# A new order of all steps, with the small matrix products in longer rows of one tile shape

## The chip, the cores and the metric

The kernel runs on one core of a Trainium2 chip. The metric is the device time in microseconds (us) of one execution, as the median of several runs. The profile is one execution taken by the hardware profiler.

## The reference

Two parts follow each other. The first is a recurrence over 768 time steps for 4 x 8 heads with states of 40 x 40; the second is a feed-forward block (FFN) with an exact gelu on 3072 tokens of width 320 and an inner width of 2048. All is float32.

```python
for t in range(S):                                   # S = 768, B = 4, H = 8, D = 40
    y[:, :, t] = einsum('bhd,bhde->bhe', rt, state)
    Sa = einsum('bhde,bhe->bhd', state, at)
    state = state * wt[:, :, None, :] - einsum('bhd,bhe->bhde', Sa, bt)
    state = state + einsum('bhd,bhe->bhde', vt, kt)
x = y.transpose(0, 2, 1, 3).reshape(B * S, H * D)    # 3072 x 320
h = x @ w_in                                         # 320 x 2048
out = (0.5 * h * (1 + erf(h / sqrt(2)))) @ w_out     # 2048 x 320
```

## The kernel before

The recurrence is cut into 12 chunks of 64 steps. Within a chunk it becomes matrix products over the 32 heads (four 64-row or 64-column quarters of the TensorE array each work on another head), with the inverse of a triangular 64 x 64 matrix for each head. After each chunk its 256 tokens go through the FFN.

The kernel is a set of step functions, one for each kind of work, and each takes the chunk's number. A step is a generator: it issues a few instructions, yields, and goes on when it is called again. One long string, ORDER, names the steps by hand, token for token (`A7:2` is the next piece of step A of chunk 7, with PSUM buffer 2), and a loop calls them in that order. So ORDER sets the order of the instructions on every engine (TensorE, VectorE, ScalarE, GpSimd and the DMA queue of SyncE, called SP), and which of four PSUM buffers (duo0 to duo3, two banks each) a product uses. No scheduler changes it. Semaphores make each instruction wait for the data and the buffers that it needs; within an engine all stays in order.

```python
for token in ORDER.split():
    name, *at = token.split(":")
    places[:] = [int(x) for x in at]
    if name not in going:
        kind = name.rstrip("0123456789")
        going[name] = steps[kind](int(name[len(kind):]))
    next(going[name], None)
```

The steps of a chunk c, with the lines that stand for them in the profile:

- Loads by SP: w, a, b, k, v, r (L213, L224, L227, L239, L266, L277). Later chunks are loaded in pairs of rows, so that VectorE can turn them: L561 is its transpose, in ta, tb, tk, tv, tr and wt.
- logs, sums and wt: the decays. ScalarE takes Ln and Exp (L499, L522, L542, L547, L549), VectorE the running sum (L544, a scan).
- ta, tb, tk: operands scaled by the decays (L588 makes aT, L614 nT, L631 kT). sc and sk scale rows of b and k (L597, and L605 on GpSimd).
- N, A, RV: small products of these operands, 32 each of 64 x 64 (TensorE, L149, the helper of all small products), each masked by VectorE out of PSUM (L676).
- The inverse of N: the mask's result goes to DRAM (L715), comes back as blocks of 32 x 32 (nb, L784), GpSimd inverts them (inv, L799 and L801, 31 rounds), the result goes to DRAM (L808), and ft loads it into the tile Tt (L822, L826). Then corner (VectorE transpose L908, small products, ScalarE copy L916) and joined (small products of tile shape 32 x 32, then a copy by ScalarE and one by VectorE, both L931) fill in the missing quarter of Tt.
- av, X: small products, added up in avs (L760, L943). sa and saT multiply avs by Tt; saT's result goes to the tile late (L980, L981), sa's to SM (L968). tn transposes the state (L557, then L997), M is a masked product of late with rT.
- yy, QY, qk: 32 small products each, added up in two PSUM buffers; y multiplies them into xt (L1045) and SP moves some rows of xt (L1071, L1076); state brings the state up to date (L1091, L1092).
- ph: the first FFN product, 160 products in four pieces with the tile shape 64 x 128 (L1119), gelu by ScalarE (L1122).
- po: the second FFN product with the full shape 128 x 128. Chunks 0 and 1 take it plainly (L1141); the others by seven products of half the size (L1157) with sums by VectorE before and after (L1164, L1172, L1184, L1185, L1161) and copies by ScalarE (L1174, L1175, L1187). The result is stored by SP (L1131).

Before chunk 2 the weights, which come as 64-bit floats, are made into float32 by VectorE and ScalarE (ci and co, L457 to L473). The first chunk's inverse is made on TensorE instead (sq, cornerd, joinedd).

The tile shape of a small product is 64 x 64 rows and columns of the array, but 32 x 32 in corner and joined. A float32 product appears in the profile as two matmul records, a transpose as one.

Of the kernel before, what the change touches and what calls it, by code (L numbers as in the profile page):

```python
# [29 lines left out]
ORDER = """  # L30
w0 begin6 pads1 consts0 w1 tails1 b1 inv1 zeros1 begin6:0 logs0 zeros2 wi0 gaps0 b0 consts0 logs1 tails0 pads0 a0
consts0 sums0:1 gaps1 sums0:2 zeros0 v0 sums0 zeros4 warm6:3 pads3 pads2 sums1:0 zeros3 shifts0 sums0 sc0 a1 sums1:3
sums1 tb0:2 sums1 sc1 wi0 ta0:1 r0 tb0 ta0 tb1:3 N0:0 N0 tb1 wi0 ta1:2 k0 ta1 N0 tv0:1 sq1 v1 tv0 sq0 N1:3 sq0 sq0:0
sq1 sq0 sq1:2 k1 sq0 sq1 warm1:1 N1 sq1 sk0 ci0:0 wi0 sq1:0 N1 ci0 sq1 tr0:1 sq1 ci0 tk0:2 wi0 tk0 sk1 wi0 sq0:3 sq1
sq0 tr0 A0:2 ci1:1 sq1:0 sq0 ci1 sq1 sq0 nb1 sq1 A0 sq1 wi0 sq0:1 wi0 sq0 RV0:3 sq0 RV0 sq0 wl1 sq1:0 wl1 sq1 inv1 r2
sq0:2 sq1 sq1 sq0 tk1:1 sq0 sq0 sq1:3 tk1 w2 sq1 sq0:0 sq0 cornerd0 placed2 av0:2 ci2:2 placed3 cornerd0:3 ci1 ci2
inv1 nb1 placed1 warm0:1 cornerd0 wl0 ci3:0 wl0 av0 av0:0 r1 ci2 joinedd0:1 av0 joinedd0 tr2:3 placed0 joinedd0 tr2
warm2:2 wi1 a2 ci3 sa0:0 sa0 sa0:1 inv1 sa0 b2 warm5:2 ci4:1 ci9:2 ci4 QY0:3:0 logs2 ci4 k2 qk0 warm7:2 ci9 y0 warm3:1
wi1 state0 wi1 A1:2 wi1 A1 wi1 sums2:1 wi1 inv1 ci9 wo2 sums2:0 sums2 ci3 tv1:3 tv1 tr1:2 sc2 sums2 tn1:0 ci5:1 tn1
ta2:3 ta2 ci5 av1:1 tr1 ci5 sk2 inv1 y0:0 tb2:3 wi1 inv2 ci7:2 tb2 wo6 zeros6 y0:2 ci7 zeros7 y0 y0 tk2:3 av1 ci6:0  # L40
N2:2 ci6 N2 ft1 tk2 co3:1 ph0:0 ft1 ci6 wi1 ph0 corner1:0 N2 ci7 X1:1 corner1:2 corner1 ft1 ph0 X1 ph0:3 wo0 ci8:0
co2:2 ci8 RV1:2 RV1 nb2 warm4:1 ci8 joined1:0 wo9 joined1 wq3 ph0 co0:0 joined1 co0 inv2 ph0 co0 v2 ph0:1 co2 co3
co1:0 sa1:2 co1 sa1 w3 co1 saT1:0 saT1 co3 ph0 co2 wo4 ph0 inv2 ph0:3 co6:0 wt3:1 co6 co7:2 ph0 vp3 co7 ph0 co7
yy1:2:0 logs3 M1:1 M1 tv2:3 wt3 co6 wo8 sums3:1 nb2 sums3 wt3 QY1 zeros5 a3 inv3 tv2 qk1 co4:2 y1 wo15 po0:1 inv2
co5:0 y1 state1 co5 co4 po0 co5 RV2:3 wo10 A2:0 co4 y1 tn2:2 A2 tn2 co9:0 po0 ta3 co9 wt3 inv2 co15:2 bp3 po0 co9 co15
av2:0 co11:1 kp3 co8:0 co11 av2 co11 ph1:2 co8 co8 wo14 inv2 ph1 co10:1 tb3 co10 ph1 wo13 ph1:0 co10 a4 ph1 RV2 ph1
inv4 ft2 co14:0 ph1:2 ta3 co14 wo12 ft2 co14 ft2 N3:3 co15 X2:0 k4 X2 ph1 corner2:1 co13:0 corner2:0 N3 corner2 co13
co12:2 N3 po0 co13 co12 joined2:0 tables0 joined2 k3 joined2 po0 ta4 ph1 co12 sa2:3 nb3 tables0 saT2:0 tk3:1 b3 sa2
sk3 saT2 po0 r3 inv3 yy2:2:3 po0 po0 M2:0 po0 nb3 M2 po0 tv3 ph1:1 inv3 po0 tr3 wq4 ph1 sc3 QY2 w4 qk2 y2 po1:0 state2
bp4 inv3 po1 logs4 b4 A3:2 y2 A3 X3:3 wt4:0 po1 wt4 v3 ph1 wt4 po1 y2 inv3 wt4 po1 po1 ta4 kp4 po1 inv3 vp4 av3:2 tb4  # L50
av3 sums4:1 po1 X3 po1 RV3:2 v4 ws0 sums4 N4:3 N4 inv5 sk4 RV3 ph2:1 N4 sc4 tk4:2 ph2 ft3 ph2 ft3 ph2:3 ws3 nb4 ws1
nb4 ph2 corner3:1 ph2 ft3 ph2:2 inv4 a5 corner3:1 corner3 w5 ph2 ph2 joined3:3 joined3 r4 tn3:1 joined3 tn3 inv4
saT3:3 saT3 sa3:2 sa3 logs5 po1 ph2:1 ta5 bp5 yy3:3:2 M3:0 M3 inv4 tv4 ph2 ph2 tr4 wq5 QY3 qk3 po2:0 po1 sums5:0 sums5
y3 po1 po2:1 state3 y3 po2 inv4 wt5:2 RV4:0 po2:1 po2 wt5 k5 A4:2 po2 A4 tn4:3 y3 tn4 wt5 po2:1 tables1 wt5 po2 po2
inv4 kp5 av4:2 tb5 av4 X4:3 po2 ph3:2 sk5 X4 a6 po2 ta5 ph3 v5 RV4 N5:3 N5 ws2 po2:1 N5 po2 ft4 po2 ph3 ft4 ph3:0 ft4
corner4:0 nb5 tk5:2 ph3 vp5 ph3 corner4:3 ta6 corner4 inv5 nb5 po2 po2:1 po2 joined4:2 joined4 joined4 ph3:0 b5 saT4:3
saT4 sa4:1 r5 inv5 sa4 ph3 ph3 sc5 ph3:2 w6 yy4:3:1 M4:0 M4 tv5 ph3 inv5 ph3 tr5 wq6 QY4 logs6 po3:1 qk4 bp6 state4
po3:0 kp6 y4 po3 po3:2 wt6:0 A5:2 po2 sums6:1 A5 wt6 inv6 k6 inv5 sums6 wt6 y4 po3 wt6 po3 po3:3 po3 po3 tn5:2 y4 tn5
av5:1 tb6 RV5:0 po3 av5 po3 po3:2 ta6 b6 po3 inv5 po3 a7 N6:1 X5:3 N6 X5 N6 sk6 ph4:2 RV5 tk6:1 ph4 ph4 ft5 ta7 ph4:1
ft5 sc6 ft5 A6:3 corner5:0 nb6 r6 inv6 po3 po3:0 po3 corner5:2 A6 corner5 ph4 joined5:0 joined5 ph4 joined5 ph4:2 vp6  # L60
sa5:3 sa5 saT5:0 saT5 inv6 ph4 nb6 ph4 yy5:1:3 w7 M5:0 tr6 tv6 ph4:2 M5 wq7 ph4 inv6 ph4 QY5 v6 logs7 po4:2 qk5 po3 y5
bp7 po4:0 wt7:1 state5 wt7 po4 kp7 po4:0 av6:2 inv7 av6 y5 inv6 wt7 po4 po4 po4:1 wt7 po4 po4 v7 sums7:3 X6:2 y5 po4
ta7 sums7 tb7 po4 po4:0 po4 a8 X6 N7:3 inv6 N7 RV6:1 tk7:2 N7 ph5:2 po4 k7 ph5 ph5 ph5:3 ft6 nb7 ph5 ft6 ph5 nb7
# [22 lines left out]
y11 po10:0 y11 po10 po10 y11 po10 y11 po10 po10:2 y11 y11 y11 po10 y11 po10 po10 po10:1 po10 po10 ph11:3 ph11 ph11
ph11:0 ph11 ph11 ph11:2 ph11 ph11 ph11:1 ph11 ph11 po11:0 po11:3 po11 po11:2 po11 po11 po11:0 po11 po11 po11 po11
po11:2 po11 po11 po11 po11:1 po11 po11
# [1179 lines left out]
```

## Time and profile before

| | |
|---|---|
| runs | 662.33, 666.8 and 668.32 us; median 666.8 us |
| span of the profiled execution | 661.8 us (its own time is not listed apart from the three runs) |
| TensorE | busy 646.7 us, weight loads 567.3 us, 13768 matmuls |
| VectorE | busy 416.0 us, 536 instructions |
| ScalarE | busy 239.3 us, 305 instructions |
| GpSimd | busy 367.7 us, 799 instructions |
| DMA | 79.41 MB, queue q1 with 58.3% of 16 engines' time |

The span goes from the first to the last instruction. A busy TensorE isn't TensorE at its peak: the ends of matmuls are modelled. The granted TensorE clock was 0.999 over the span. In the rows, `<-` in a tile pair stands between what is written and what is read, and behind `<-` in an idle time stands what ended it; "duo" is any of the four PSUM buffers.

### The profile page before, as it was taken

What the parts mean: (1) busy time and instruction counts of PE and PEld (TensorE: products, weight loads), DVE (VectorE), ACT (ScalarE), POOL (GpSimd) and SP (SyncE); (2) the same over time, 40 slices, a digit from 0 to 9 for tenths busy, and PEclk for the clock granted to TensorE, in tenths of its full rate; (3) what the DMA queues carried; (4) which work ended last, traced back from release to release, by engine and by line L of the source; (5) the groups of instructions that cost most, each with busy time, mean ns of one, the idle gap of its engine ahead of it and who ended that gap; (6) DMA issues with size and microseconds to landing.
All of it is one profiled execution on the core that took longest, in us unless ns stands there. A gap on an engine that the chain in (4) does not pass through costs nothing.

```text
span 661.8 us, 30753 instructions
## 1 busy us (share of the span) xinstructions
PE 646.7 (98%) x13768; PEld 567.3 (86%) x13768; DVE 416.0 (63%) x536; ACT 239.3 (36%) x305; POOL 367.7 (56%) x799
## 2 busy tenths in 40 slices
...
GB/s 136 164 192 176 158 167 132 153 159 146 116 132 134 105 137 134 140 116 112 145 141 107 94 153 124 119 147 110 115 146 111 103 121 102 86 101 3 42 1 21
DMA packets 300708, 79.41 MB, mean 120 GB/s; under 512 B 288584, under 2 KB 293328, under 8 KB 300576
## 3 DMA queue, kind: packets, MB, share of 16 engines
q1 hardware_dynamic: 299512, 74.92, 58.3%
q0 software_dynamic: 864, 2.36, 1.8%
...
q14 instruction: 24, 0.20, 0.1%
q10 hardware_dynamic: 200, 0.16, 0.1%
...
## 4 chain that ended last, share of the span: by engine, by line
PE 82%; DVE 8%; SPq 5%; issue 2%; DMA 1%; ACT 0%; DVEq 0%; ACTq 0%
PE duo L1119 29%; PE duo L149 25%; PE duo L1157 22%; PE duo L1141 4%; PE duo L557 2%; SPq L213 2%; SPq L227 1%; DVE conv L466 1%; SPq L1076 1%; DVE conv L472 1%; DMA spare<-in_a_dram 1%; DVE conv L458 1%; DVE conv L457 1%; DVE aT L588 1%; DMA rows<-in_b_dram 0%
## 5 line engine op out<-in xcount | busy, mean ns | idle before, releaser
L1119 PE MATMUL duo<-xt,w_in_sb 64*128 64x256 f32 x1920 | 218.8, 381 | 1.4 <-issue 1.4
L1119 PEld LDWEIGHTS duo<-xt,w_in_sb 64*128 64x128 f32 x1920 | 182.5, 187 | 23.9 <-issue 2.3
L799 POOL TENSOR_TENSOR tmp<-W,Nb 128x56 f32<-128x56 f32 (+22 forms) x155 | 71.8, 464 | 79.9 <-DMA Nb<-N 51.4
L1122 ACT ACTIVATE gt<-duo 128x1024 f32<-128x1024 f32 x48 | 49.2, 1025 | 143.0 <-PE duo L1119 132.1
L799 POOL TENSOR_TENSOR tmp<-rT,Nb 128x56 f32<-128x56 f32 (+22 forms) x155 | 70.2, 453 | 52.8 <-DMA Nb<-N 41.0
L1157 PE MATMUL duo<-w_out_sb,gt 128*128 128x160 f32 x640 | 93.3, 303 | 0.0
L1157 PEld LDWEIGHTS duo<-w_out_sb,gt 128*128 128x128 f32 x640 | 87.6, 190 | 2.4 <-issue 0.8
L801 POOL TENSOR_TENSOR W<-W,tmp 128x56 f32<-128x56 f32 (+22 forms) x155 | 71.8, 463 | 12.1
L801 POOL TENSOR_TENSOR rT<-rT,tmp 128x56 f32<-128x56 f32 (+22 forms) x155 | 68.4, 441 | 12.1
L1157 PE MATMUL duo<-extra,conv 128*128 128x160 f32 x320 | 46.0, 301 | 0.0
L1157 PEld LDWEIGHTS duo<-extra,conv 128*128 128x128 f32 x320 | 43.8, 190 | 1.4 <-issue 0.5
L1141 PE MATMUL duo<-w_out_sb,gt 128*128 128x320 f32 x128 | 36.9, 440 | 0.1
L1161 DVE TENSOR_TENSOR os<-os,duo 128x160 f32<-128x160 f32 x40 | 12.7, 318 | 31.9 <-PE duo L1157 28.0
L1141 PEld LDWEIGHTS duo<-w_out_sb,gt 128*128 128x128 f32 x128 | 23.6, 190 | 10.1 <-issue 0.5
L1164 DVE TENSOR_TENSOR conv<-gt 128x1024 f32<-128x1024 f32 x10 | 12.7, 1266 | 27.5 <-ACT gt L1122 27.5
L605 POOL TENSOR_TENSOR rows<-rows,w_tile 128x640 f32<-128x640 f32 x9 | 15.8, 1761 | 25.0 <-DMA Nb<-N 16.0
L676 DVE TENSOR_TENSOR SM<-duo,left_upper 128x1024 f32<-128x1024 f32 x11 | 13.4, 1221 | 24.4 <-PE duo L149 24.4
L931 DVE COPY Tt<-duo 32x512 f32<-32x512 f32 x11 | 7.6, 689 | 30.4 <-ACT Tt L931 30.3
L149 PE MATMUL duo<-rT,late 40*64 40x64 f32 x1472 | 26.1, 219 | 0.0
L149 PEld LDWEIGHTS duo<-rT,late 40*64 40x64 f32 x1472 | 23.7, 135 | 2.1 <-issue 2.1
L1122 ACT ACT_TABLE_LOAD x14 | 18.0, 1283 | 19.1 <-DVE os L1161 14.7
L1157 PE MATMUL duo<-extra,gt 128*128 128x160 f32 x160 | 23.9, 302 | 0.0
...
## 6 DMA issues: line engine op xcount, KB each, us to landing
...
```

The costliest lines, as they stand in the source:

```text
L149: nc.tensor.matmul(o, lhsT, rhs, start=first, stop=True, skip_group_check=True)
L213: nc.sync.dma_start(out=t[half(e)].rearrange("p g h d -> p (g h) d")[:, :, :D], in_=rows_of(src, c, e))
L557: nc.tensor.transpose(pt[:, g, n], src(g, n), ident)
L605: (nc.gpsimd if c in SCALED_BY_POOL or c >= NB else nc.vector).tensor_tensor(to, raws.pop((c, "k")), t["rw"], ALU.mult)
L676: nc.vector.tensor_tensor(to, pt, upper.unsqueeze(1).to_broadcast([P, NBL, C]), ALU.mult)
L799: eng.tensor_tensor(t, W[:, :nr, j:j + 1].to_broadcast([P, nr, rest]), Nb[:, j:j + 1, j + 1:].to_broadcast([P, nr, rest]), ALU.mult)
L801: eng.tensor_tensor(W[:, :nr, j + 1:], W[:, :nr, j + 1:], t, ALU.add)
L1119: nc.tensor.matmul(pt[:, x, s], w_in_sb[half(x), kt, p * P:(p + 1) * P], xt[half(x), kt], start=kt == 0, stop=kt == NK - 1)
L1122: nc.scalar.activation(gt[:, 4 * q:4 * q + 4].rearrange("p (x s) t -> p x s t", x=2), pt, ACT.Gelu)
L1141: nc.tensor.matmul(pt[:, g], gt[:, f, g * P:(g + 1) * P], w_out_sb[:, f], start=f == 0, stop=f == NF - 1)
L1157: nc.tensor.matmul(pt[:, n, :DM // 2], l_[:, f], r_[:, f], start=f == 0, stop=f == NF // 2 - 1)
L1161: nc.vector.tensor_tensor(to, one_, other, ALU.add)
```

## The change

ORDER alone is replaced by another string of the same steps; no function changes. All steps of all chunks, and with them the instructions and DMAs of all engines, stand in another order, and many tokens have another PSUM buffer. Each step is called as often as before. Small products of one tile shape are gathered: before, single small products alternate with pieces of ph and po; after, several pieces of one step and several small products follow each other. Here is the stretch around chunk 7 in both strings; the rest is changed in the same way.

```diff
-corner6:0 ph5:0 RV6 ft6 inv7 corner6:2 po4 corner6 tn6:3 r7 tn6 po4:1 po4 joined6:2 ta8 joined6 joined6 ph5 inv7 vp7
-ph5 sa6:3 sa6 saT6:1 saT6 ph5:2 po4 yy6:0:3 bp8 M6:1 M6 inv7 tr7 ph5 ph5 tv7 QY6 po5:1 wq8 qk6 y6 po5:1 state6 y6 po5
-po5:2 inv7 po5 wt8:0 A7:2 y6 RV7:0 A7 wt8 tn7:3 RV7 tn7 wt8 vp8 inv7 po5 po5:1 po5 wt8 po5 X7:2 av7:0 inv8 av7 tb8 sk7
-kp8 po5 ta8 b7 inv9 po5 po5:3 po5 a9 po5 N8:0 N8 ft7 ph6:1 N8 ph6 ph6 ft7 ta9 ph6:3 ft7 corner7:1 X7 ph6 tk8:2 nb8 ph6
...
+X6:2 po4 N7:0 inv7 ph5:1 ph5 ph5 X6 ph5:2 inv8 sc6 N7 ph5 N7 ph5 ph5:1 ft6 ft6 corner6:1 ph5 nb7 ft6 ph5 corner6:2 vp7
+tn6:0 corner6 joined6:1 joined6 RV6:2 sk6 w7 tn6 tk7:0 inv7 ta8 inv7 r7 joined6 saT6:3 saT6 sa6:0 RV6 nb7 inv7 yy6:2:1
+k7 logs7 M6:3 sa6 tv7 wq8 M6 ph5:0 ph5 A7:3 ph5 A7 tables1 po5:0 QY6 qk6 av7:3 po5:0 po5 y6 state6 po5:1 po5 tr7 tn7:1
+wt8:2 wt8 po5 po5:0 po5 tn7 bp8 y6 b7 po5 kp8 y6 wt8 po5 po5 po5:1 po5 wt8 tb8 av7 a9 po5 po5 po5:0 sums7:1 X7:3 inv7
+ta8 sums7 N8:2 po5 inv7 b8 N8 sc7 N8 ft7 RV7:1 ph6:0 ta9 ph6 ph6 ph6:2 ph6 ph6 ph6:0 ph6 X7 po5 corner7:2 corner7:2
```

More of the change, by code (lines that the diff above doesn't have):

```diff
@@ L36 @@
[L36 to L50, printed above, removed]
@@ L86 @@
[L86 to L88 removed]
+zeros0 begin6 begin6:0 tails0 w0 consts0 w1 a0 pads2 logs0 b0 pads1 a1 b1 zeros3 wl0 sums0:0 sums0:1 v0 logs1 sums0
+consts0 sums1:2 sums1:3 sums1 pads0 k0 zeros1 wi0 pads3 sc0 gaps0 ta0:1 sums0 warm4:3 tb0:0 tb0 sums1 warm5:3 ta0 sc1
@@ new lines @@
+N0:1 N0 ta1:2 N0 sq0 zeros2 sq0 warm0:0 tb1:1 tb1 sq1 r0 sq0:0 sq1 ta1 sq1:3 sq1 wi0 wi0 wi0 gaps1 N1:1 inv1 N1 N1 sq1
+sk0 sq0 sq1:2 k1 sk1 sq1 sq1 tk0:3 sq0 sq0:0 tails1 sq0 v1 sq0 nb1 sq1 tv0:2 sq1:1 sq0 tk0 sq0:3 sq1 sq0 sq1 sq1 ci0:0
+ci1:1 tr0:0 shifts0 sq0 sq1:1 sq1 tv0 A0:2 ci1 sq0 sq1 wl0 sq0:3 sq0 wi1 wi1 sq1 sq1:1 sq0 tr0 RV0:0 A0 sq1 sq0 nb1
+zeros4 RV0 sq0:3 tk1:2 av0:1 tv1:0 sq0 ci0 ci0 tk1 inv1 cornerd0 ci5:0 cornerd0:2 ci1 placed3 placed0 wi0 inv1 placed1
+wi0 wi0 b2 inv1 ci4:2 ci2:1 w2 av0 av0:1 wi1 inv1 cornerd0 joinedd0:2 ci4 wi0 warm7:3 placed2 joinedd0 wi1 wi1
@@ new lines @@
+joinedd0 sa0:3 r2 sa0 av0 sa0:1 sa0 tv1 ci5 A1:0 A1 ci4 warm2:3 QY0:1:2 qk0 logs2 sums2:0 sums2:3 state0 y0 ci3:2
+sums2 a2 y0:1 y0:2 ci2 r1 sc2 wl1 ci3 wi1 k2 ci2 y0 y0 av1:3 X1:2 sums2 wi1 wi1 ci5 ta2:0 ta2 warm1:1 tables0 av1 X1
+ci6:0 wl1 tr2:3 inv1 tb2:1 tb2 wo0 tables0 ci3 tr1:0 ci7:1 tr2 ci6 ci6 N2:2 ci7 N2 ph0:1 ph0 consts0 tr1 ci9:0 ci9 ci7
+RV1:0 sk2 tk2:2 ph0 ph0:3 ph0 ci8:2 ci8 ph0 ci9 ci8 ph0:1 N2 co1:0 ph0 co1 tk2 ft1 corner1:2 wo6 ph0 RV1 tn1:0
+corner1:2 ft1 corner1 nb2 co7:2 ft1 co0:1 wo2 A2:1 zeros7 ph0:2 A2 tn1 co0 co0 co1 joined1:1 co7 joined1 joined1 co3:0
@@ new lines @@
+co3 w3 ph0 co2:1 ph0 saT1:1 saT1 co2 wo4 yy1:0:3 v2 co3 co6:0 co2 sa1:2 sa1 zeros6 inv2 M1:1 M1 co6 po0:2 nb2 co7 co6
+co4:2 zeros5 QY1 co5:0 co5 wq3 co4 qk1 a3 inv2 tv2:1 y1 po0 wo9 state1 av2:3 co4 tv2 co5 y1 wt3:2 logs3 wo10 RV2:1
+inv2 y1 av2 sums3:0 X2:3 inv2 wt3 po0 ta3 inv2 wo8 bp3 RV2 sums3 tn2:1 po0 wt3 wt3 co11:0 co11 co10:1 co11 co9:2 wo14
+wo15 co10 co8:0 inv2 X2 co10 tb3 tn2 co14:1 ta3 co8 co9 a4 co9 co14 co8 ph1:0 ph1 ph1 ph1:1 ph1 ph1 ph1:3 ph1 co15:2
+co15 co14 co15 ft2 N3:0 wo12 N3 po0 po0 corner2:2 co12:1 co12 corner2:0 ft2 ft2 ph1 ph1:1 wo13 N3 co12 kp3 co13:2 co13
@@ new lines @@
+corner2 ph1 joined2:0 inv3 joined2 co13 v3 po0 po0 ph1 joined2 nb3 saT2:0 po0 vp3 tk3:2 r3 A3:3 po0 saT2 sa2:2 yy2:0:1
+A3 sa2 M2:3 po1:2 po1 M2 QY2 qk2 nb3 tv3 av3:3 av3 ta4 po0 wq4 ws0 po1 po1 bp4 k3 state2 inv3 inv3 wt4:2 tr3 b3 inv3
+po0 po1 po1 po1 po1 wt4 y2 y2 wt4 wt4 tb4 X3:1 y2 ta4 N4:0 ph2:3 po1 inv3 kp4 N4 ph2 a5 N4 inv3 ws1 ph2 ph2:0 ph2 ph2
+ph2:3 ws3 po1 ws2 ph2 ph2 tk4:2 ph2:0 po1 po1 nb4 nb4 ph2 ft3 X3 ft3 ft3 corner3:2 corner3:3 tn3:1 corner3 ph2 sc3
+joined3:3 joined3 vp4 RV3:2 v4 tn3 joined3 saT3:0 r4 RV3 sa3:1 sa3 saT3 inv4 A4:2 A4 sk3 w4 inv4 yy3:0:3 M3:1 po2:2 M3
@@ new lines @@
+po2:2 po2 tv4 wq5 po2:1 QY3 tr4 po2 k4 logs4 av4:2 av4 po2 qk3 ta5 y3 wt5:0 po2:1 po2 wt5 po2 po2 bp5 y3 kp5 po2 po2:2
+wt5 state3 po2 inv4 y3 warm3:0 wt5 tn4:3 tn4 tb5 sums4:1 ta5 v5 po2 sums4 RV4:0 po2 X4:3 N5:1 N5 ph3:2 inv4 inv4 inv4
+N5 ph3 ph3 inv6 ph3:1 ph3 inv5 a6 X4 ft4 ft4 RV4 ft4 corner4:0 ph3 ph3:2 ph3 corner4:1 corner4 po2:0 tk5:1 ph3
+joined4:1 A5:2 joined4 joined4 nb5 sa4:3 A5 b4 saT4:1 saT4 av5:2 po2 sa4 vp5 yy4:3:0 inv5 ta6 M4:1 r5 tv5 av5 M4 sc4
+ph3:2 ph3 nb5 QY4 sk4 ph3 wq6 po3:1 w5 qk4 k5 wt6:0 y4 wt6 state4 po3:2 po3 po3:2 po3 po3 po3:0 po3 po3 logs5 po2 b6
@@ new lines @@
+wt6 tr5 tn5:2 tn5 bp6 v6 inv5 po3 y4 po3 po3:3 y4 wt6 tb6 ta6 a7 po3 po3 inv5 po3 po3:0 sums5:2 N6:3 N6 inv5 inv5 N6
+kp6 X5:1 sums5 ft5 b5 ta7 sk5 ph4:2 ph4 tk6:0 sc5 ph4 corner5:0 ph4:3 ph4 nb6 X5 ph4 ph4:2 ph4 ph4 ph4:3 ft5 ph4 ph4
+ft5 po4:2 corner5:1 warm6:2 corner5 joined5:1 vp6 w6 RV5:3 r6 joined5 joined5 po3 saT5:2 saT5 RV5 nb6 sa5:0 logs6
+yy5:3:1 sa5 inv6 M5:2 po4:0 po4 po4:0 tv6 inv6 po4 M5 A6:2 inv6 inv6 tr6 sums6:0 wq7 kp7 sums6 QY5 A6 wt7:1 qk5 po3
+av6:0 bp7 k6 po4 po4:2 po4 po4 wt7 v7 y5 wt7 state5 y5 av6 wt7 tb7 ta7 po4 po4 po4:0 y5 po4 po4 a8 inv6 po4 po4:1 po4
@@ new lines @@
+sk7 ft7 corner7 tk8:1 RV7 ph6 ph6:1 ph6 ft7 joined7:0 joined7 nb8 joined7 A8:2 ph6 saT7:3 saT7 nb8 r8 A8 sa7:1 sa7 k8
+vp8 yy7:2:0 inv9 M7:3 po6:1 po6:1 M7 QY7 tv8 qk7 v8 av8:3 po6 y7 w8 state7 po6:2 po6 wq9 inv8 wt9:0 po6 logs8 po6:0
+wt9 po6 po6 wt9 av8 tn8:3 po6 tn8 inv8 tr8 bp9 y7 inv8 wt9 po6 vp9 po6:1 y7 kp9 tb9 inv8 po6 ta9 po6 po6 po6:0 po6
+sums8:3 inv8 N9:2 sums8 ph7:1 N9 N9 ph7 tk9:0 a10 ph7 ph7:2 ph7 ph7 ft8 ft8 sc8 ft8 ph7:1 ph7 corner8:0 corner8:2
+corner8 nb9 nb9 X8:0 joined8:2 joined8 RV8:3 X8 A9:0 joined8 saT8:2 RV8 k9 sk8 A9 ph7 po6 sa8:3 v9 inv9 ta10 yy8:0:1
@@ new lines @@
+sa8 saT8 inv9 M8:2 M8 ph7:3 ph7 ph7 QY8 w9 qk8 r9 tv9 wq10 tr9 po7:0 y8 wt10:2 av9:3 wt10 b9 state8 kp10 po7:2 po7
+po7:1 logs9 po7 po7 po7:0 po7 po7 tn9:2 tn9 bp10 inv9 po7 po7 y8 y8 k10 wt10 wt10 tb10 a11 av9 po7:1 po7 ta10 po7 inv9
+inv9 po7 po7:0 X9:2 X9 RV9:3 po7 po7 N10:1 RV9 N10 ft9 sums9:2 sums9 sk9 N10 tk10:2 ft9 ft9 nb10 ph8:0 sc9 ta11 ph8
+ph8 ph8:1 ph8 ph8 ph8:0 corner9:2 corner9:1 corner9 ph8 vp10 joined9:1 joined9 A10:2 ph8 joined9 saT9:3 nb10 saT9 A10
+sa9:0 yy9:2:1 M9:3 sa9 ph8:0 inv10 inv10 ph8 M9 QY9 qk9 ph8 inv10 v10 w10 logs10 tv10 state9 wq11 av10:0 bp11 y9 po8:2
@@ new lines @@
+po8:3 po8 po8:1 po8 wt11:0 r10 y9 tn10:1 tn10 po8 y9 wt11 k11 po8:3 po8 po8 po8 inv10 inv10 wt11 tr10 po8 po8:1 po8
+wt11 tb11 av10 kp11 ta11 v11 po8 po8 po8:3 po8 N11:0 X10:3 RV10:1 N11 sums10:0 ph9:2 ph9 sums10 ph9 inv10 N11 b10
+ph9:0 RV10 X10 ph9 ft10 b11 inv11 nb11 ft10 corner10:0 sc10 ph9 ph9:2 ph9 ph9 ph9:0 ft10 tk11:1 corner10:2 corner10
+ph9 po8 joined10:2 joined10 sk10 w11 inv11 inv11 A11:3 joined10 A11 saT10:1 ph9 saT10 sa10:0 po9:1 sa10 yy10:3:2 M10:1
+vp11 tv11 M10 nb11 po9:0 po9 QY10 po9:0 logs11 qk10 sums11:1 po9 y10 po9 po9:0 po9 state10 po9 po9 y10 inv11 po9
```

42 lines of the change are left out of this document (6 added, 36 removed).

## The prediction

> **What bounds the kernel now.** I read the page first: its span, the busy time of the engines and the chain that ended last.
>
> ```profile
> span 661.8 us, 30753 instructions
> ...
> PE 646.7 (98%) x13768; PEld 567.3 (86%) x13768; DVE 416.0 (63%) x536; ACT 239.3 (36%) x305; POOL 367.7 (56%) x799
> ...
> PE 82%; DVE 8%; SPq 5%; issue 2%; DMA 1%; ACT 0%; DVEq 0%; ACTq 0%
> ```
>
> TensorE (PE) carries 82% of the chain. Whether that holds in every stage is told by the table of windows, and by the waits of PE from 209 us to 658 us.
>
> ```profile
> 0.00:100.00 100.00, 91.89 (x2072) 72.36 (x2074) 72.38 (x115) 49.70 (x66) 52.97 (x138) 1.00 0.89 166
> 100.00:208.00 108.00, 105.65 (x2119) 84.71 (x2119) 79.46 (x117) 42.37 (x55) 63.09 (x143) 1.00 0.69 140
> 208.00:400.00 192.00, 191.53 (x4401) 173.65 (x4394) 130.78 (x144) 67.97 (x85) 125.55 (x254) 1.00 0.63 125
> 400.00:600.00 200.00, 200.00 (x4403) 182.94 (x4403) 116.44 (x135) 70.93 (x87) 126.10 (x266) 1.00 0.58 113
> ```
> ```profile
> PE duo L149 <- DVE aT L588: 0.4, 1, 0.4
> ```
>
> The second column is PE's busy time: all of its idle time lies before 208 us (8.1 and 2.4 us). From there to the end PE waits once, for 0.4 us. So a change of order can win in the steady part only by making PE's own row of work shorter, and it can lose by any wait that it brings in, because there is none now.
>
> What can be shorter is shown by the chain in order of time (start, length, line, number of matmul records).
>
> ```profile
> 155.27 1.09 PE duo L149 x64
> ...
> 209.31 2.36 PE duo L1119 x20
> ...
> 219.70 4.54 PE duo L1157 x32
> 224.25 2.02 PE duo L149 x128
> ...
> 227.30 4.35 PE duo L1157 x32
> ...
> 337.73 10.99 PE duo L1119 x100
> ```
>
> Equal pieces cost different times, and what differs is what stands before them. The 32 records at 219.70 follow small products and take 4.54 us; the 32 at 227.30 follow transposes of the same full tile shape and take 4.35. So entering the full shape (128 x 128) costs 0.19 us. For line 1119 (64 x 128), 100 records in one go take 10.99, 20 alone 2.36: (10.99 - 2.36) / 80 = 0.108 a record, 20 of them 2.16, and the entry 0.20. For small products (64 x 64) 128 records take 2.02 and 64 take 1.09: 64 more cost 0.93, the entry 0.16.
>
> **The change, part by part.** It is a new order only: every instruction and every DMA is issued as often as before. I counted, in the order of PE's instructions, the stretches of one tile shape: 212 now, 140 in the changed kernel. By shape: 128 x 128 from 64 to 40, 64 x 128 from 41 to 23, 64 x 64 from 80 to 50; 32 x 32 (24) and 128 x 64 (3) stay.
>
> *Term 1, fewer entries.* 24 x 0.19 + 18 x 0.20 + 30 x 0.16 = 4.6 + 3.6 + 4.8 = 13.0 us (bounds 12.3, if the four at the start are hidden, and 13.4). 68 of the 72 stretches saved lie behind the first 110 us of PE's work, where PE doesn't wait, so no wait hides this gain.
>
> *Term 2, the inverse's last copies.* Longer rows of small products mean less FFN work between a small product and the one that needs its result. The tightest place is from "joined" (Tt<-Js) to "saT" or "sa", which read Tt:
>
> ```profile
> 204.80 0.75 PE L149 MATMUL duo<-Tt,Js 32*32 32x32 f32 x64
> ...
> 205.49 1.10 PE L557 MATMUL duo<-ident,st 128*128 128x128 f32 x8
> ...
> 205.84 0.56 ACT L931 COPY Tt<-duo 32x512 f32<-32x512 f32 x1
> ...
> 206.43 0.69 DVE L931 COPY Tt<-duo 32x512 f32<-32x512 f32 x1 [6.51 <-ACT Tt L931]
> ...
> 207.18 1.16 PE L149 MATMUL duo<-Tt,avs 64*64 64x64 f32 x62 [0.59 <-DVE Tt L931]
> ```
>
> The two copies run one after the other, though on two engines: from 205.49, where PE is through with "joined", to 207.18 are 1.69 us. Here 1.1 us of transposes stood between, and PE sat idle 0.59. Now ten chunks have 2.5 us or more of PE work there and this one 1.2. In the changed order seven chunks (3 to 7, 9 and 10) have a single row of small products there, 0.93 + 0.16 = 1.09 us: seven waits of 0.6 for one. Cost 6 x 0.6 = 3.6 us; bounds 2 (if the entry overlaps the wait) and 5.
>
> *Term 3, VectorE at a chunk's end.* After QY and qk, VectorE (DVE) has y, the state, the scan of the next decay and, behind them, the aT (L588) that the next N needs. PE stands still at N, and behind it stand X, the sums and the next FFN part, which are what ScalarE and the chain of states wait for. These are its rows:
>
> ```profile
> L544 DVE TENSOR_TENSOR_SCAN conv<-going_on,conv 128x1024 f32<-128x1024 uint8 x9 | 21.3, 2369 | 3.0 <-ACT conv L542 3.0
> L1045 DVE TENSOR_TENSOR xt<-duo,wpT 128x512 f32<-128x512 f32 x24 | 15.4, 685 | 8.4 <-PE duo L149 8.4
> ...
> L588 DVE TENSOR_TENSOR aT<-aT,wpT 128x1024 f32<-128x1024 f32 x9 | 13.6, 1514 | 6.4 <-ACT wpT L549 6.4
> L676 DVE TENSOR_TENSOR SM<-duo,left_upper 128x1024 f32<-128x1024 f32 x11 | 13.4, 1221 | 24.4 <-PE duo L149 24.4
> L1185 DVE TENSOR_TENSOR gt<-gt 128x1024 f32<-128x1024 f32 x10 | 13.4, 1336 | 0.0
> L1184 DVE TENSOR_TENSOR gt<-gt,conv 128x1024 f32<-128x1024 f32 x10 | 13.2, 1322 | 0.0
> L1161 DVE TENSOR_TENSOR os<-os,duo 128x160 f32<-128x160 f32 x40 | 12.7, 318 | 31.9 <-PE duo L1157 28.0 <-ACT os L1187 3.5
> L1172 DVE TENSOR_TENSOR conv<-conv,gt 128x1024 f32<-128x1024 f32 x10 | 12.7, 1269 | 0.1
> ...
> L1092 DVE TENSOR_TENSOR st<-st,wpT 128x320 f32<-128x320 f32 x20 | 12.3, 617 | 0.7
> ...
> L561 DVE STREAM_TRANSPOSE nT<-a_pairs 128x1024 f32<-128x1024 f32 x9 | 11.2, 1244 | 4.5 <-PE duo L149 4.5
> ...
> L614 DVE SCALAR_TENSOR_TENSOR nT<-nT,kT 128x1024 f32<-128x1024 f32 x9 | 11.0, 1227 | 0.6
> ...
> L1091 DVE TENSOR_TENSOR st<-duo,st 128x320 f32<-128x320 f32 x20 | 9.6, 479 | 0.5 <-PE duo L149 0.5
> ```
>
> The first figure after the bar is the group's time, the second the mean of one in ns. For the changed order's first steady chunk end they add up, from y to aT, as 2 x 0.685 + 1.244 + 1.322 + 1.336 + 0.318 + 2.369 + 2 x (0.479 + 0.617) + 1.244 + 1.227 + 1.514 = 14.1 us. Seven chunk ends in a row, counted alike, give 14.1, 15.8, 9.9 (+ 2.3 left of L1184 and L1185 just before), 18.5, 17.0, 15.8 and 16.1. PE's work between the end of qk and N, which must cover that, is 13.2, 17.0, 13.1, 18.9, 15.8, 19.2 and 17.4 (now 19.3, 18.4, 16.6, 18.7, 21.5, 22.5 and 23.4, against 17.8, 14.8, 13.0, 17.9, 14.8, 15.2 and 16.0: always less work than cover, and hence no wait). To DVE's sums come about 0.4 us of hand-over and three adds of L1161 (1.1) that free N's or X's PSUM tile. Work less cover: 2.4, 0.3, 0.6, 1.1, 2.7, none, 0.2: 7.3 us. If the adds come late enough not to count, 3; if every end costs the worst of them, 2.7, it is 19.
>
> The Trainium skill ("TensorEngine Tiling (Array Packing)", section "PSUM Bottleneck") speaks against this change too: small tiles speed up TensorE but not the emptying of PSUM, and the copy may become the bound. The rows agree as to size (0.93 us for a product of 64 records, 1.22 for its mask in L676); by the rule alone each product that DVE masks would put it 0.29 us behind in a row, which is part of the queue counted above.
>
> *Term 4, the start.* Conversion of the weights fills DVE up to about 150 us. Counted with mean times, DVE's queue stands at most 17.8 us behind PE's order in the changed kernel, 12.7 now, both near 130 us, but the later queue holds more that PE needs late. I take 1 us; bounds 0 and 5.
>
> *Sum.* 661.8 - 13.0 + 3.6 + 7.3 + 1.0 = 660.7. The profiled execution's own time is not listed apart; its span lies 0.5 below the lowest and 5.0 below the median (666.8) of the three runs. With 5.0 around it: **665.7 us**, 0.2% under the median. The three runs spread over 0.9%, so about 1% can be told from no change.
>
> **The rivals.**
>
> *A, faster: the entries are saved and VectorE keeps up.* DVE is busy 63%, and may start its transposes and products before qk ends wherever their inputs are there; then term 3 falls away. For it: DVE's 130.78 us in 192 leave a third free. Against it: the order is strict within an engine, and aT stands behind y and the state. Time: 661.8 - 13.0 + 3.6 + 1 = 653.4, with 5.0: 658.4. If term 2 falls too, 654.8.
>
> *B, slower: the round trip of the inverse becomes the bound.* N goes to DRAM, comes back as blocks, GpSimd inverts, and ft loads Tt, all issued in one strict SP queue.
>
> ```profile
> 290.16 1.21 DVE L676 TENSOR_TENSOR N<-duo,left_upper 128x1024 f32<-128x1024 f32 x1
> ```
> ```profile
> 346.47 0.71 DVE L908 STREAM_TRANSPOSE conv<-Tt 128x512 f32<-128x512 f32 x1 [4.72 <-DMA Tt<-inv]
> ```
>
> From mask to corner that is 56.3 us, and DVE already waited 4.72 for the load. With N's row and hand-overs before and the transpose behind, 58.4. PE's work from N to corner is 61.1 at its shortest in the steady part of the changed order (60.2 now), but terms 2 and 3 delay the masks by 1 to 2.7 us. Past 61.1 corner is late; at 1.5 us in each of nine chunks, 13.5 more: 674.2, with 5.0 679.2. The upper end of term 3 alone gives 660.7 + 11.7 + 5.0 = 677.4, also slower.
>
> *C, the entries aren't won.* If an entry cost time because of something else that now moves elsewhere (a weight load that finds its tile late), the sum lacks term 1. The equal pieces above, always the same to 0.02 us, speak against it; 660.7 + 13.0 + 5.0 = 678.7.
>
> **How the numbers follow.** Forecast 665.7 with 42%, A 30%, B with the dear end of term 3 25%, C 3%. So faster by over 1% 0.30, within 1% 0.42, slower 0.28. The range goes from A without term 2 (654.8) to just past term 3's dear end: 654 to 678; the forecast's own range, with 3 to 10 for term 3, is 661 to 669.
>
> **What would show it.** Right: in the changed chain pieces of 32 records of L1157 mostly at 4.35 and few at 4.54; in PE's waits after 209 us about 0.6 us for DVE Tt L931 in seven chunks and 0.3 to 2.7 for DVE aT L588 or os L1161 in five or six. Term 1 is wrong if pieces of a shape cost less when entered; term 3 if those waits are missing (A) or above 2.7 each; B is right if PE or DVE L908 waits for DMA Tt<-inv by more than 4.72 in several chunks. The forecast is wrong if PE's idle time after 209 us is under 5 or over 17.

## The result and the profile after

The changed kernel takes 731.08 us (median; 726.56 to 734.78) against 665.55 for the kernel before in the same measurement: a ratio of 1.097, 95% interval 1.091 to 1.104. The forecast was 665.7 us in a range of 654 to 678. The change costs some 65 us, and the prediction missed the cause altogether.

The profiled execution has a span of 731.2 us, 69.4 more than before. These are the page's span, busy times, instruction queue (packets, MB, share of the DMA engines) and chain:

```profile
span 731.2 us, 30759 instructions
...
PE 675.3 (92%) x13768; PEld 597.9 (82%) x13768; DVE 406.5 (56%) x536; ACT 235.2 (32%) x302; POOL 344.0 (47%) x799
...
PEclk9999998998997999999998998997999999898999
...
q8 instruction: 108, 1.77, 1.1%
...
PE 84%; issue 7%; DVE 6%; ACT 1%; DMA 1%; SPq 1%; POOL 0%; DVEq 0%; POOLq 0%; ACTq 0%
```

Two things are new. "issue", time in which an engine waited for nothing that the profile shows, has gone from 2% to 7% of the chain. And PEclk, which was at full speed all along, has dips from the seventh slice on. The table of windows, with the prediction's bounds from 208 us on, shows how much (busy time of PE with its matmul records, the same of the others, then clock, DMA share, GB/s):

```profile
208.00:400.00 192.00, 177.65 (x4013) 161.44 (x4012) 103.75 (x119) 62.80 (x77) 112.57 (x251) 0.95 0.64 122
400.00:600.00 200.00, 183.87 (x3883) 170.47 (x3876) 115.06 (x135) 60.39 (x77) 98.01 (x226) 0.95 0.59 111
600.00:731.00 131.00, 121.86 (x2010) 113.01 (x2006) 40.36 (x57) 25.42 (x36) 27.58 (x65) 0.95 0.19 39
```

Behind 208 us PE now idles 14.4 + 16.1 + 9.1 = 39.6 us. Of these, 4.1 lie behind its last product, where the order before idles 4.2; up to the last product 35.5 stand against 0.5. Its clock is 0.95 there: 5% of 523 us are another 26 (28.6 by the trace's clock records). These two make most of the loss, and they are spread over all chunks. What ends the idle time, from 208 us to the end (total, times, longest):

```profile
PE duo L149 <- issue: 32.1, 24, 2.2
PE duo L1157 <- issue: 1.5, 2, 1.1
PE duo L149 <- DVE Tt L931: 1.3, 6, 0.2
PE duo L1119 <- issue: 0.4, 1, 0.4
PE duo L149 <- DVE os L1161: 0.2, 1, 0.2
```

34.0 of 35.5 us have no releaser: no data, no buffer, no DMA that the kernel knows of. The waits that the prediction added up (L931, and VectorE's queue at a chunk's end) come to 1.5 us. One such stretch, chunk 3's row of small products, in the chain in order of time:

```profile
221.22 2.29 PE duo L149 x122
223.51 1.85 issue
225.36 3.42 PE duo L149 x125
228.78 0.58 issue
229.36 1.98 PE duo L149 x57
231.34 6.84 PE duo L1157 x32
```
```profile
225.70:235.90 10.20, 9.62 (x197) 9.31 (x189) 6.88 (x6) 0.00 (x0) 8.87 (x18) 0.50 0.46 87
```

PE runs 122 records of small products, stands still 1.85 us in the middle of a step whose other products had already begun, runs 125, and stands still again; between the two restarts lie 4.00 us. (The chain leaves out some records that overlap. In the trace, 128 matmul records, each with its weight load, lie between these two restarts: 256 instructions.) Then the window shows the clock at 0.50 for 10.2 us, and the 32 records of L1157 behind the row take 6.84 us instead of 4.54.

The instruction queue's row explains the number. 108 packets of 1.77 MB are 16,384 bytes each. PE has 13768 + 13768 = 27536 instructions in the page, 107.6 times 256. So each packet brings 256 of PE's instructions. A row of small products uses them up in 1.87 us (128 records at 14.58 ns, the 0.93 us for 64), an FFN piece of L1119 (40 instructions in 2.16) would take 14. My theory after the result: **TensorE is handed 256 instructions per some 4 us at most; the longer rows of the new order ask for more; and the gaps then bring the clock down.** The rivals: the waits of the prediction (VectorE, loads, the inverse), in a form that the profile puts down to "issue" wrongly.

The Trainium skill bears on both halves of this theory. Its page "Runtime: NRT & Kernel Launch", section "Instruction fetch mechanics", says that instructions come in blocks of 256 while the block before runs, and that crossing a block's end is mostly hidden; the rows above speak against "hidden", with 1.85 and 0.58 us. The Trainium skill's page "TensorE: Matmul & The Clock Gate", section "Part 1: The HAM clock gate", says that after an idle window of about 3.4 us the clock halves. The 10.2 us at 0.50 are three such windows, so the trace agrees as to length; but no gap behind 208 us is longer than 2.2 us, so here the clock halves without a wholly idle window.

### The profile page after: what moved, and what is told of

It is laid out like the page before. It is cut to its first block, busy times and chain, and to the rows that moved or that the text cites. A ratio compares the mean times of both kernels' runs of the same rounds, so it can differ in the third digit from the quotient of the medians.

```text
span 731.2 us, 30759 instructions
## 1 busy us (share of the span) xinstructions
PE 675.3 (92%) x13768; PEld 597.9 (82%) x13768; DVE 406.5 (56%) x536; ACT 235.2 (32%) x302; POOL 344.0 (47%) x799
## 3 DMA queue, kind: packets, MB, share of 16 engines
q8 instruction: 108, 1.77, 1.1%
## 4 chain that ended last, share of the span: by engine, by line
PE 84%; issue 7%; DVE 6%; ACT 1%; DMA 1%; SPq 1%; POOL 0%; DVEq 0%; POOLq 0%; ACTq 0%
PE duo L1119 29%; PE duo L149 27%; PE duo L1157 21%; PE duo L1141 5%; PE duo L557 2%; DMA rT<-in_k_dram 1%; DVE conv L472 1%; DVE conv L466 1%; DVE Tt L931 1%; DVE aT L588 0%; ACT Tt L931 0%; DVE conv L457 0%; DVE conv L544 0%; DVE conv L458 0%; DVE os L1161 0%
## 5 line engine op out<-in xcount | busy, mean ns | idle before, releaser
L1119 PE MATMUL duo<-xt,w_in_sb 64*128 64x256 f32 x1920 | 222.6, 388 | 0.6 <-issue 0.4
L1119 PEld LDWEIGHTS duo<-xt,w_in_sb 64*128 64x128 f32 x1920 | 190.6, 193 | 26.3 <-issue 2.7
L799 POOL TENSOR_TENSOR tmp<-rT,Nb 128x56 f32<-128x56 f32 (+22 forms) x155 | 65.1, 420 | 95.7 <-DMA Nb<-N 84.2
L1157 PE MATMUL duo<-w_out_sb,gt 128*128 128x160 f32 x640 | 100.1, 317 | 1.1 <-issue 1.1
L799 POOL TENSOR_TENSOR tmp<-W,Nb 128x56 f32<-128x56 f32 (+22 forms) x155 | 67.5, 436 | 70.5 <-DMA Nb<-N 58.8
L1157 PEld LDWEIGHTS duo<-w_out_sb,gt 128*128 128x128 f32 x640 | 95.8, 204 | 2.4 <-issue 1.5
L801 POOL TENSOR_TENSOR W<-W,tmp 128x56 f32<-128x56 f32 (+22 forms) x155 | 65.1, 420 | 12.1
L801 POOL TENSOR_TENSOR rT<-rT,tmp 128x56 f32<-128x56 f32 (+22 forms) x155 | 64.4, 415 | 12.2
L1157 PE MATMUL duo<-extra,conv 128*128 128x160 f32 x320 | 45.7, 300 | 0.4 <-issue 0.4
L1157 PEld LDWEIGHTS duo<-extra,conv 128*128 128x128 f32 x320 | 43.9, 190 | 1.3 <-issue 1.0
L149 PE MATMUL duo<-rT,late 40*64 40x64 f32 x1472 | 33.3, 237 | 12.2 <-issue 12.2
L149 PEld LDWEIGHTS duo<-rT,late 40*64 40x64 f32 x1472 | 29.4, 150 | 14.5 <-issue 14.1
L1141 PEld LDWEIGHTS duo<-w_out_sb,gt 128*128 128x128 f32 x128 | 25.7, 206 | 10.8 <-issue 2.3
L931 DVE COPY Tt<-duo 32x512 f32<-32x512 f32 x11 | 7.6, 689 | 46.7 <-ACT Tt L931 46.7
L908 DVE STREAM_TRANSPOSE conv<-Tt 128x512 f32<-128x512 f32 x11 | 7.8, 705 | 39.1 <-DMA Tt<-inv 39.1
```

The costliest lines, as they stand in the source:

```text
L149: nc.tensor.matmul(o, lhsT, rhs, start=first, stop=True, skip_group_check=True)
L799: eng.tensor_tensor(t, W[:, :nr, j:j + 1].to_broadcast([P, nr, rest]), Nb[:, j:j + 1, j + 1:].to_broadcast([P, nr, rest]), ALU.mult)
L801: eng.tensor_tensor(W[:, :nr, j + 1:], W[:, :nr, j + 1:], t, ALU.add)
L931: copy(F[lo[q], :, BL:].rearrange("p (n z) t -> p z n t", z=2), J[lo[q]])
L1119: nc.tensor.matmul(pt[:, x, s], w_in_sb[half(x), kt, p * P:(p + 1) * P], xt[half(x), kt], start=kt == 0, stop=kt == NK - 1)
L1141: nc.tensor.matmul(pt[:, g], gt[:, f, g * P:(g + 1) * P], w_out_sb[:, f], start=f == 0, stop=f == NF - 1)
```

## Experiments: is it the number of instructions?

**Half the instructions, nearly the same work (e2, e3).** One pair of records with doubled columns in place of two, in both orders:

```diff
-            for n in range(NP):
+            for n in range(0, NP, 2):
...
-                        mm(pt[half(e ^ j if swap else e), j, g, n], lT[half(j, D), g, n, e],
-                           rT[half(j, D), g, n, e])
+                        mm(pt[half(e ^ j if swap else e), j, g, n:n + 2], lT[half(j, D), g, n, e],
+                           rT[half(j, D), g, n:n + 2, e])
```

> The changed order, but every small product of two neighbouring heads is one instruction pair with twice the columns in place of two pairs (odd heads get the even head's left operand, so the values are others): half the instructions, nearly the same time on the array (estimated 19 us less in all, from 14.58 ns for a record of 40 or 64 columns and 22.28 for 104). All loads, all work of VectorE, ScalarE and GpSimd, the order, the buffers and the 140 stretches stay. Theory (instruction supply): the gaps of 1 to 2.4 us and the halved clock vanish; 640 to 660 us, within 15 us of the kernel before with the same edit. Rival (VectorE, ScalarE, loads or buffers are late in the new order): these are as late as before, 715 to 731 us, and some 60 us more than the kernel before with the same edit.

> The same edit (half the instructions for small products, the columns doubled; other values) on the order before. Both theories: 640 to 660 us, 666 less the estimated 19 of array time plus what the round trip of the inverse, 58.4 us against shorter work between N and corner, then shows.

Measured: 660.23 us for the changed order (ratio to the kernel before 0.991, 0.988 to 0.995), 642.48 for the order before (0.965, 0.959 to 0.971). From 731 to 660 with all loads, all other engines and the order kept; 19 of these 71 us are less array time. The issue waits of PE are gone from the changed order's list behind 208 us, and the instruction queue has 71 packets; these are its page's row and its waits:

```profile
q8 instruction: 71, 1.16, 0.8%
```
```profile
PE duo L149 <- DVE os L1161: 4.5, 5, 2.1
PE duo L1157 <- DVE st L1091: 4.0, 3, 1.5
PE duo L149 <- DVE aT L588: 1.4, 3, 0.6
PE duo L149 <- DVE Tt L931: 1.4, 7, 0.3
```

So the number of instructions decides, as the theory says. But the two orders lie 17.8 us apart, past the 15 expected: now that PE isn't starved, waits of the kind that the prediction had added up appear. In the changed kernel PE is late itself, and its gaps seem to cover them.

**More work at no cost (e4).** Fillers of 0.88 us of array time and few instructions ahead of later products of a row:

```diff
+            for j in range(2):
+                mm(pt[half(e), j], ident[half(e ^ j if crossed else j), :HP],
+                   cum_m[half(e ^ j if crossed else j)].unsqueeze(1).to_broadcast([HP, 4, P]))
...
-joined6 saT6:3 saT6 sa6:0
+joined6 fill16:3 saT6:3 saT6 fillx17:0 sa6:0
```

> The changed order with 43 fillers: four products of 512 columns in the small tile shape, 0.88 us of work on the array in 16 instructions, put ahead of the third and each later small product of a row, into the buffer that this product takes anyway. Nothing reads them. Added array work 37.8 us. Theory (instruction supply): the work falls into the gaps, and with less idle time the clock drops less often: 690 to 735 us, no longer than without the fillers. Rival (data or buffers late): the work stands in the row of TensorE's work and comes on top, about 760 to 769 us.

Measured: 729.87 us. The 37.8 us of added work (an estimate: 43 fillers of 0.88) cost nothing in sum; the rival asked for 760 or more. These are its mean clock, against 0.95 in the windows of the changed kernel, and PE's main wait behind 208 us:

```profile
core 0: 727.6 us, clock 0.992
```
```profile
PE duo L152 <- issue: 23.5, 29, 1.4
```

The gaps are shorter (1.4 us at most, 23.5 in all, where they were 2.2 and 32.1), and the clock stays up. So the fillers took the place of some 10 us of gaps and of most of the halved clock. Both halves of the theory show in one kernel.

**Rows by themselves (e1, e5).** Small products without any data to wait for, put into the kernel before:

```diff
+        for k in range(n):
+            e, j = k // 2 % 2, k % 2
+            at = k // 4 % (512 // width) * width
+            mm(pt[half(e), j, at:at + width], w_in_sb[half(j, D), 0, :HP], w_in_sb[half(j, D), 1, at:at + width])
```

> The kernel before, with rows of small products (64 x 64 tile, four quarters in turn, no data to wait for) added: 512 products with 64 columns in the middle of the run, and behind the end 1024 with 64 columns, 1024 with 128 and 512 with 256, with eight wide products between the rows. Nothing reads these rows. Theory (TensorE is handed 256 instructions per 4.0 us at most, and a product is four instructions): gaps every 256 instructions in the rows with 64 columns; 1024 products take about 64 us, against 29.9 by the array (29.16 ns each); with 128 columns 60 to 64 us against 56; with 256 columns no gaps, 56 us. The row in the middle takes 28 to 32 us against 15. Rival (the stalls after the change come from data or buffers of the new order): no gaps, 30, 56 and 56 us, 15 in the middle.

> The kernel before, with rows of small products (64 x 64 tile, no data to wait for, nothing reads them) put between two pieces of the FFN: 64, 128, 256 and 384 products with 64 columns in chunks 2, 3, 5 and 6, 256 and 128 products with 128 columns in chunks 7 and 8. Behind the end 1024 products with 64 columns with no loads under way, 1024 with 64 while the loads of 12 tiles in rows of 160 bytes run, and 1024 with 128 columns under such loads. Theory (256 instructions per 4.0 to 4.5 us, a short lead of some 1.5 us at the start of a row): beyond the array's time 64 products cost 0 to 1 us, 128 some 2 to 3, 256 some 6 to 8, 384 some 10 to 14, and the halved clock shows from 128 on; 256 products with 128 columns cost at most 2.4, 128 at most 1.2. Behind the end: 58 us without loads, as measured; if loads slow the supply, 69 to 74 with them for both widths. Rival (the supply doesn't depend on loads): 57 to 60 for all three. Rival (the length of a row doesn't count, only its data): nothing beyond the array's time in the middle.

Measured, one execution each: 888.51 and 940.16 us. The row of 512 products in the middle of the first kernel took 28.4 us by its first and last record, array time 14.9. Its chain:

```profile
333.35 0.95 issue
334.30 2.10 PE duo L149 x125
336.40 2.19 issue
338.58 3.69 PE duo L149 x99
...
343.14 7.15 PE duo L149 x205
```

The restarts lie 4.28 and 4.56 us apart, without any data in play: the rival is out. In the second kernel the length counts. The chains of the rows with 128, 256 and (128 columns) 256 products:

```profile
248.82 2.48 PE duo L150 x158
251.30 1.01 issue
```
```profile
352.00 3.54 PE duo L150 x219
355.54 2.46 issue
358.00 3.69 PE duo L150 x128
```
```profile
495.03 14.13 PE duo L150 x512
```

From the first record of the row to the first behind it, the row of 64 takes 2.02 us and these three 5.16, 14.84 and 14.13; with 29.16 ns a product (54.8 with 128 columns) and 0.16 for the entry the array needs 2.03, 3.89, 7.62 and 14.2. So 64 products cost nothing extra, 128 cost 1.3 (less than expected), 256 cost 7.2, 384 (21.93 us) 10.6, and 256 with twice the columns nothing, though 256 of their instructions are only 3.5 us of work. Each length stands there once.

Three expectations failed. The 1024 products behind the end took 57.8 us in the first kernel, not 64, and 57.4 with 128 columns, not 60 to 64. In the second the loads ran earlier than meant, under the whole of the first row (61.3 us) and two thirds of the second (59.6), and the row with 128 columns had none (59.2), where 69 to 74 stood for slow loads: they change little. In the rows with 64 columns the clock is the limit. It also didn't drop for 128 products in the middle, only from 256 on. These windows hold the row with 64 columns, then that with 128 (PE busy, records, clock):

```profile
700.00:710.00 10.00, 9.93 (x371) 0.50 0.02 5
...
760.00:770.00 10.00, 10.00 (x376) 1.00 0.02 5
```

After its first gap (1.52 us) the row stays at 0.50 to its end, and at half clock 1024 products take 59.7. With 128 columns there is no gap at the start and the clock stays at 1.00: 57.4 us, where the array alone needs 56. That is 256 instructions in 3.6 us with no loads under way, so that 4.0 isn't a constant.

The trace also has the time of each packet of the instruction queue, and this settles what the rows leave to argument. In the changed kernel, behind 208 us, 23 small products start over 0.55 us after the record before them. Each of these starts comes 2.3 to 3.0 us after the start of a packet, and where two follow each other in one row they are 127 or 128 matmul records and 3.4 to 4.3 us apart. The restarts at 225.36 and 229.36 follow packets that start at 222.95 and 226.40; those at 334.30, 338.58 and 343.14 in the first kernel of rows follow packets at 331.96, 336.06 and 340.62. The packets themselves come at least 3.3 us apart in every run, and 3.7 on average in the first kernel's rows of 1024 products with 64 and with 128 columns. Whether the loads make the difference to the 3.4 to 4.6 of the running kernels isn't settled.

## Experiments: the waits that the prediction named

**VectorE's running sum (e7).** Only 128 of 1024 columns, on top of e2:

```diff
-        nc.vector.tensor_tensor_scan(plain(logs_of), going_on, plain(logs_of), 0.0, ALU.mult, ALU.add)
+        nc.vector.tensor_tensor_scan(plain(logs_of)[:, :2 * HP], going_on[:, :2 * HP], plain(logs_of)[:, :2 * HP], 0.0, ALU.mult, ALU.add)
```

> The changed order with half the instructions for small products, as in the run e2_after_half, and besides with VectorE's running sum (L544, 2.37 us for each chunk from 3 on) over 128 of its 1024 columns alone, so that the decays have other values. It asks what the 18 us between the two orders with half the instructions are. If VectorE's queue at the end of a chunk (term 3 of the prediction) makes most of them: TensorE's waits for DVE os, st and aT, 9.9 us in that run, fall under 4 and the time to 650 to 655 us. If it is late loads, the clock or short rests of the instruction supply: 658 to 661 us, no change.

Measured: 656.05 us, 4.2 under e2 (ratios 0.982, 0.976 to 0.988, and 0.991, 0.988 to 0.995: they just touch). The waits for os, st and aT fall from 9.9 to 5.3:

```profile
PE duo L1157 <- DVE st L1091: 3.4, 2, 2.2
PE duo L149 <- DVE os L1161: 1.9, 2, 1.5
```

By the waits VectorE's queue is part of the 18 us, but the times alone hardly show it, and neither expectation is met; the rest stays open.

**A shorter inverse (e8).** 8 of 31 rounds on GpSimd from chunk 3 on, in the changed order:

```diff
+            if c < 3 or j < 8:
-            eng.tensor_tensor(t, W[:, :nr, j:j + 1].to_broadcast([P, nr, rest]),
+                eng.tensor_tensor(t, W[:, :nr, j:j + 1].to_broadcast([P, nr, rest]),
```

> The changed order, with 8 of the 31 rounds of the inverse on GpSimd from chunk 3 on (other values in Tt; loads, stores and the rest as they were), which takes some 20 us from the 56 between N's mask and corner. If the round trip of the inverse (rival B of the prediction) makes TensorE late in the changed order, below 700 us. If the supply of instructions and the clock make the loss, no change: 724 to 733 us.

Measured: 737.46 us (1.102, 1.093 to 1.110), not faster. GpSimd's rounds don't bound the changed kernel; PE's first row is the same as after:

```profile
PE duo L149 <- issue: 32.7, 22, 2.2
```

## Experiments: breaking the rows up again

Pieces of the FFN are put back into the rows; the rest keeps the changed order. e9 has e8's inverse besides. Of e10, around chunk 7:

```diff
-ft7 corner7 tk8:1 RV7 ph6 ph6:1 ph6 ft7 joined7:0 joined7 nb8 joined7 A8:2 ph6 saT7:3 saT7 nb8 r8 A8 sa7:1 sa7
+ft7 corner7 tk8:1 RV7 ft7 ph6 joined7:3 ph6 joined7 nb8 joined7 A8:2 ph6:1 saT7:3 saT7 nb8 r8 A8 sa7:0 ph6 ph6 sa7
```

> The changed order with pieces of the FFN moved back into the rows of small products (and buffers renamed where that needs it): 194 stretches of one tile shape against 140 after the change and 212 before; all instructions of VectorE, GpSimd and the DMA queues stay in the changed order, only some gelu move with their pieces. A count of instructions with 256 per 4.0 us and a lead of 64 instructions gives 13.1 us of gaps for it, against 56.6 for the changed order and 1.3 for the order before. Theory (instruction supply, then the clock): 731 - 43.5 of gaps + 9.9 of entries = 697, and less what the clock gives back, up to 26: 670 to 697 us. Rival (the order of the other engines makes TensorE wait): 731 + 9.9, about 735 to 745 us.

> The order of e6_after_spread (pieces of the FFN back in the rows of small products) with the same 8 of 31 rounds of the inverse. In e6 TensorE's gaps without a releaser fell from 34 us behind 208 us to 3, but it waited 28.4 us for VectorE's L908, which waited for the inverse, since the pieces came out of the stretch between N and corner that covers the round trip. If that is the whole reason why e6 was slow: 755 - 28 - some 15 to 25 of halved clock behind these waits, 695 to 715 us. If the order of VectorE and ScalarE holds TensorE back in other places as well: 735 or more.

> The changed order with fewer pieces of the FFN moved into the rows: those alone that leave the work between N and corner above 59.5 us, and the copies between corner, joined and saT their time. 174 stretches; by the count of instructions 34.0 us of gaps (56.6 in the changed order, 13.1 in e6). Theory (supply, then the clock): 731 - 22.6 + 6.2 of entries - some 14 of the clock = 701, 693 to 720 us. Rival (other engines): 731 to 745.

> As e10_after_spread_less (pieces of the FFN moved into the rows; 176 stretches, by the count of instructions 33.9 us of gaps against 34.0 there and 56.6 in the changed order), but the pieces between N of a chunk and corner of the chunk before it stay: at least 11 us of TensorE's work. In e9 SP's strict queue held the inverse's load behind the store of the next N, and from N's mask to corner it took 10.4 us, so that these pieces cover it. If that is what e10 lost beside the supply (4.8 us of waits for L908, 3.2 for os, and the clock behind them): 703 to 718 us. If the other waits come from something else: 720 to 728, as e10.

Measured: 755.20 us (1.129, 1.121 to 1.137), 756.56 (1.133, 1.124 to 1.142), 723.45 (1.085, 1.078 to 1.092) and 725.20 (1.085, 1.077 to 1.094). The theory's times failed in all four: e6 is slower than both of its readings, e9 and e11 fell to the other one, e10 is 3 us above the theory's range. What the theory says of the gaps did come: rows of PE's waits behind 208 us in e6, e10 and e11.

```profile
PE duo L149 <- DVE conv L908: 28.4, 4, 10.0
...
PE duo L149 <- issue: 3.1, 3, 1.2
```
```profile
PE duo L149 <- issue: 15.9, 12, 1.9
PE duo L149 <- DVE conv L908: 4.8, 3, 2.5
```
```profile
PE duo L149 <- issue: 14.7, 13, 1.9
PE duo L149 <- DVE conv L908: 5.2, 2, 4.4
```

From 32.1 us of issue in the changed order to 3.1 in e6 and half in e10 and e11: fewer instructions in a row, fewer gaps. But each piece that is moved uncovers something else. In e6 that is above all the load of the inverse, and my reading of it, that the inverse is too slow, was wrong: with a quarter of its rounds (e9, where the transpose is L909) nearly the same wait stands there. The wait's row in e9, and the chain behind one of its four times, show what it is (L715 stores N, L227 loads a later chunk's a, L823 loads the inverse):

```profile
PE duo L149 <- DVE conv L909: 26.1, 4, 10.1
```
```profile
499.12 1.15 DVE spare L676
...
500.28 0.32 SPq L715
...
503.11 0.49 SPq L227
...
505.35 0.37 SPq L823
...
505.76 2.93 DMA Tt<-inv
...
508.82 0.72 DVE conv L909
```

The load of one chunk's inverse stands in SP's strict queue behind the store of the next chunk's N, which waits for N's mask. From the mask's start to the transpose's end pass 10.4 us, with GpSimd's rounds cut to a quarter, and in the order before FFN pieces between N and corner cover such a stretch. The wait that ends at 399.19 us in e9 has the same store ahead of it; the other two stand outside the chain. e11 kept at least 11 us of work there and gained nothing over e10, so in these two kernels the remaining waits for L908 have another reason, which wasn't tried. No order tried here beats the kernel before.

## Why the prediction was wrong

**The step that failed** is the one that all others stood on: "it can lose by any wait that it brings in", where waits were looked for among data, buffers and queues alone. The instructions themselves were not in the sum. The prediction counted stretches of one tile shape, but not how many instructions a stretch asks for and how fast they come. What the runs showed in its place: TensorE gets 256 instructions per packet, no faster than one in 3.3 us and in the long rows one in 3.4 to 4.6, while 256 instructions of small products are 1.87 us of work. The profile before had the signs: a row for the instruction queue, and a block of 256 instructions with under 3 us of work stands alone there, between longer ones, and costs nothing.

**The term that is missing**, sized: I gave each block of 256 instructions its work time by the prediction's own rates and entries and took it from the block's measured time. Behind 208 us nearly nothing is left over in the order before (0.7 us in all), 69.2 in the changed one: 35.5 of gaps and waits, 28.6 of halved clock (it is halved for 57.1 us there), and some 5 whose cause is open. Ahead of 208 us it is 17.8 and 31.8. The rates leave 1 or 2 us of play in each figure. With the entries saved the account is -13.2 + 68.5 + 14.0 = 69.3 of 69.4 us.

**Term 1 (entries, 13.0) was right.** Pieces of the changed kernel that no gap precedes:

```profile
293.06 8.89 PE duo L1157 x64
...
302.83 6.52 PE duo L1157 x48
...
311.90 17.47 PE duo L1119 x160
```

64 records of L1157 behind small products take 8.89 in one go, where twice 32 took 9.08; 48 behind transposes 6.52, three halves of 4.35; 160 of L1119 0.108 each and 0.20. So rival C is out: the entries are saved where TensorE isn't held up.

**Terms 2 and 3 (3.6 and 7.3)** were 1.3 and 0.2 us in the changed kernel, for PE was late itself. With the gaps taken away (e2) they were 1.4 and 9.9: term 2 was mis-sized (0.2 us a time, not 0.6), term 3 lies inside its bounds of 3 to 19, though e2 also has 19 us less array work to cover VectorE with.

**Term 4 (1.0, at most 5)** was too small. Ahead of 208 us 14.0 us more are lost. With half the instructions in both orders, some 8 to 10 us more are still lost there by the same account, so that part seems no matter of supply.

**The 5.0 us added around the span** were also mis-sized: the profiled execution of the changed kernel took 733.13 us with a span of 731.2, 1.9 more.

**Rival B** named the right wait and a wrong sign. This is VectorE's wait in the changed kernel, from the list of all waits:

```profile
DVE conv L908 <- DMA Tt<-inv: 39.1, 7, 8.3
```

It is 39.1 us in 7 times, up to 8.3, and a wait past 4.72 in several chunks was what the prediction took as proof. Yet no wait of PE for it stands in the list behind 208 us, and e8 gains nothing. A wait counts only where PE stands at its end.

**The last test spoke against the forecast, as it should:** PE's idle time behind 209 us was to stay between 5 and 17, and it is 35.5 up to the last product.
